# Spreading the key sums z by two 16-row products, and projecting v of tile 14 in the first part

## The chip, the cores and the metric

The kernel runs on one core of a Trainium2 chip. The metric is the device time of one execution in microseconds, as the median of several runs: 389.65 before the change (three runs, 389.32 to 390.35). All times below are in microseconds, and times of the trace count from the start of the span. The engines are named as in the profile: PE is TensorE (PEld its weight loads), DVE is VectorE, ACT is ScalarE, POOL is GpSimd, SP is SyncE, which issues most of the DMAs.

## What is computed

The input x has 2048 rows of 512. Two branches read it and a gate mixes them:

```
g   = sigmoid(sum(x * gate_w))                    # one number per row
out = g * A(x) + (1 - g) * B(x)

A:  q, k, v = x @ wqkv, 32 heads of 16
    phi(t) = [softmax(t @ w_phi), softmax(-(t @ w_phi))]        # 32 features per head
    kv = sum over rows of phi(k)^T v ;  z = sum over rows of phi(k)
    o  = phi(q) kv / (phi(q) . z + 1e-6) ;  A = o @ wo

B:  per row and each of 32 heads: the best of 16 keys k1 and the best of 16 keys k2
    give an expert e = 16 * i1 + i2 ;  B = sum over heads of gelu(x . u[e]) * v[e]
```

z is one number per head and feature, 32 x 32 = 1024 in all. Each row of x needs all of them, multiplied with its own phi(q), so a copy of z has to lie in every one of the 128 partitions.

## The kernel before, in words

The rows are cut into 16 tiles of 128 (`NT`), and the 512 inputs into four blocks of 128 (`NK`). Operands are split into a high and a low part of the type `F32R`: `proj` (L83, over `mm3`, L51) makes twelve products of a tile, for each block high x high (L54), high x low of the weights (L55) and low of x x high (L56). All engines follow an order written out by hand: each engine executes its instructions in the order of the program text, and an instruction that waits holds everything behind it on its engine.

**The first part** (loop at L284) goes over the 16 tiles t. It projects v (`vproj`, into a tile with 17 columns per head, the last of them ones) and k (`kproj`, with w_phi folded into the weights), takes the softmax differences of k on VectorE (`softmax_diffs`, L86), the exponential on ScalarE (L326), and sums and a reciprocal on VectorE and a product on GpSimd (`ksoft`, L177 to L181), and adds phi(k)^T [v, 1] to a PSUM tile `acc` (`kvacc`, L188). Thus column 16 of each head in `acc` gathers z. Beside this the loop builds the score weights `sh`, `sl` of branch B (`score_w`, `score_planes`, `score_join`). Two tiles are treated apart: v of tiles 14 and 15 is not projected here. `kvz` (L192) adds only their z, by products with a column of ones, so that z is complete when the second part begins. In the last pass of the loop the weights of q are folded (`fold`, L133): its products go to PSUM, ScalarE rounds them to `wah` (L137), VectorE subtracts to `wal` (L138). Between its halves stand the scores of tile 0 (`front_s(0, ·)`).

**The bridge** (L627 to L641): `kvz(14)`; `best(0, ·)` finds the maxima of the scores of tile 0 on VectorE (L447) and marks them (L448); `turn_eq(0)` turns the marks by a DMA transpose on SP (L454, tile `et`); `front_q(0)` and `front_p(0)` project tile 0 on q and on u; `soft_in(0)` takes the softmax differences of q on VectorE; `kvz(15)` completes z. Then ScalarE copies z to `zc` (L638), `gelu_pre(0)` prepares the gelu, and `z_final` (L614) spreads z: for each of 8 groups of 128 numbers one 32-bit product of a column of `zc`, broadcast over 128 columns, with the identity (L618), and two copies into `zb` (L620).

**The second part** (loop at L642) runs stage a for tile a, and for n = a + 1, b = a - 1, z = a - 2: in stage a the scores of tile n are made while the softmax of q of tile a is under way, tile b is counted and turned, and tile z is finished and stored. The order of its steps around the change, in stage 0: `gate(0)` (L370) and `gelu_act(0)` (L378 to L380), then `soft_exp(0)` (L403), `mid_mask(0)` on TensorE (L511, reads `et`), `front_s(1, 0)`, `front_s(1, 1)`, `front_p(1)`, `soft_w(0)` on GpSimd (L409, needs `zb`), `soft_sum(0, ·)` (L413), `best(1, 0)`, `soft_y(0, ·)` (L417, needs the product of L409), `soft_b(0)`, `best(1, 1)`. In stage 1 TensorE also projects v of tiles 14 and 15, ScalarE copies them out of PSUM (v15 behind `soft_exp(1)`), and `kvacc(14)` and `kvacc(15)` add their part of phi(k)^T v, without the column of z; then `kv_final` copies `acc` into `kvb`. The weights wo replace those of v in the same tiles, the first two blocks by L670 and L690, the last two, whose loads wait for the buffers of the first, by L702 and L706. From stage 2 on, stage a starts on TensorE with `mid_num` (L491) and `back_c` (L563, the transpose CT of the coefficients that `coef`, L557, leaves).

PSUM is taken by two rings: `mm_bank` (four banks, in order of use) and `tr_bank` (three).

Of the kernel before, what the change touches and what calls it, by code (L numbers as in the profile page):

```python
# [9 lines left out]
F32 = mybir.dt.float32  # L10
F32R = mybir.dt.float32r
# [9 lines left out]
P = 128  # L21
S = 2048
D = 512
# [10 lines left out]
def mix_kernel(ctx, tc, xT, wqT, wkT, wv, wphi, wo, wq, kk, ug, ev, cst, out):  # L34
# [6 lines left out]
    def mm_bank(name):  # L41
        return psum.tile([P, 512], F32, tag="mm", bufs=4, name=name)
# [28 lines left out]
    ones = per.tile([P, 1], F32, name="ones")  # L71
    zc = per.tile([P, 8], F32, name="zc")
    cs = per.tile([P, 160], F32, name="cs")
    ident = cs[:, 0:128]
# [5 lines left out]
    def xs(t, k):  # L80
        return xh[:, t, k, :], xl[:, t, k, :]

    def proj(o, t, wh, wl, c0, c1, ks=range(NK)):  # L83
        mm3(o, [(*xs(t, k), wh[:, k, c0:c1], wl[:, k, c0:c1]) for k in ks], ks[0] == 0, ks[-1] == NK - 1)
# [75 lines left out]
    def vproj(t, ks=range(NK)):  # L160
        if ks[0] > 0:
            return proj(pvs.pop(t), t, wbh, wbl, 0, D, ks)
        pv = pvs[t] = mm_bank(f"pv{t}")
        proj(pv, t, wbh, wbl, 0, D, ks)
        v = vs[t] = home(t).tile([P, H, F + 1], F32, name=f"v{t}", tag="v")
        if t < NT - 2:
            pool.memset(v[:, :, F], 1.0)
        return lambda: act.copy(v[:, :, :F], pv.rearrange("p (h f) -> p h f", f=F))
# [14 lines left out]
    def kvacc(t):  # L183
        n = F + 1 if t < NT - 2 else F
        for g in range(8):
            for c in range(4):
                h = 4 * g + c
                pe.matmul(acc[32 * c:32 * c + 32, g, :n], phis[t][:, 32 * h:32 * h + 32],  # L188
                          vs[t][:, h, :n], start=(t == 0 and g == 0),
                          stop=(t == NT - 1), skip_group_check=True)  # L190
# [33 lines left out]

    def front_s(t, half):
        e = st8[t]
        e[half] = mm_bank(f"s{half}_{t}")
        proj(e[half], t, sh, sl, 512 * half, 512 * half + 512)

# [54 lines left out]
    for t in range(NT):  # L284
        if t + 3 < NT:
            x_load(t + 3)
        if 2 < t < NT - 2:
            vproj(t)()
# [111 lines left out]
    def soft_exp(t):  # L400
        d = st8[t]["ph"]
        for s_ in halves:
            act.activation(d[:, s_], d[:, s_], AF.Exp)  # L403
# [209 lines left out]

    def z_final():  # L614
        for j in range(2):
            o = mm_bank(f"z{j}")
            for g in range(4):
                pe.matmul(o[:, g * P:(g + 1) * P], zc[:, 4 * j + g:4 * j + g + 1].to_broadcast([P, P]), ident,  # L618
                          start=True, stop=True)
            act.copy(zb[:, 512 * j:512 * j + 512], o)  # L620
# [6 lines left out]
    rawo = {}  # L627
    kvz(NT - 2)
    best(0, 0)
# [7 lines left out]
    kvz(NT - 1)  # L637
    act.copy(zc, acc[:, :, F])  # L638
    gelu_pre(0)
    z_final()  # L640
    wo_load((0, 1))  # L641
    for a in range(NT - 1):  # L642
# [8 lines left out]
        if a == 1:  # L651
            v14, v15 = vproj(NT - 2), vproj(NT - 1)
        gelu_in(a)
# [6 lines left out]
        if B:  # L660
            step(b, 4)
            soft_in(a, lambda: step(b, 2))
            drain(b)
        if a == 1:
            v14()
        soft_exp(a)
        if a == 1:
# [8 lines left out]
        mid_mask(a)  # L676
        front_s(n, 0)
        if a == 1:
            kvacc(NT - 2)
            kvacc(NT - 1)  # L680
            cl_.close()
            w4 = ctx.enter_context(tc_pool("w4", "right"))
# [78 lines left out]
def _consts():  # L761
    c = np.zeros((P, 160), np.float32)
    c[:, :128] = np.eye(P, dtype=np.float32)
    p = np.arange(P)
    for q in range(2):
        for a in range(F):
            c[:, 128 + q * F + a] = np.where(p % F == a, 2.0 ** (q * 8 + p // F), 0.0)
    return c
# [42 lines left out]
```

## Time and profile before

| | |
|---|---|
| median of three runs | 389.65 (389.32 to 390.35) |
| the profiled execution | 389.51, its span 387.7 |
| granted TensorE clock, mean over the span | 0.996 |
| first z product (L618) | 135.48 |
| first score product of tile 1 (`front_s(1, 0)`) | 137.57 |
| CT transpose that opens stage 3 (L563) | 177.90 |
| mean bandwidth of the DMAs | 117 GB/s |

The page gives for each engine the time it was busy, for slices of the span the busy tenths, and the chain of work that ended last, followed back from the end: at each step to what released the instruction, or to the one before it on its engine. The timeline gives start, duration, engine, line, operation and tiles; in brackets the idle time before the instruction and what ended it. TensorE's products are pipelined: the shown duration of one is longer than the distance to the next, and a stream is measured by the distances between starts.

### The profile page before, as it was taken

Reading aid. Unit: us, or ns where it says so; the run is one execution under the profiler, and the core shown is the slowest. Engines: PE = TensorE matmul, PEld = TensorE weight load, DVE = VectorE, ACT = ScalarE, POOL = GpSimd, SP = SyncE. Lnnn points to the kernel's source line nnn. Section 1 sums busy time; section 2 is a strip of 40 time slices with the busy share of each in tenths; the row PEclk is TensorE's granted clock in tenths of the full one; section 3 lists DMA queues with packets and bytes.
Section 4 is the critical chain, followed back from the end, with each engine's and each line's share of the span. In section 5 each row is a group of like instructions: output and inputs, shape, how many; then the busy total and the mean of one; then the engine's idle time right before and its main releaser. Section 6 shows DMA issues by size and latency. Waiting matters only on the chain.

```text
span 387.7 us, 9193 instructions
## 1 busy us (share of the span) xinstructions
PE 379.2 (98%) x3688; PEld 296.4 (76%) x3688; DVE 324.3 (84%) x798; ACT 214.2 (55%) x390; POOL 155.9 (40%) x165
## 2 busy tenths in 40 slices
PE   8999999999999999999999999999999999999975
PEld 4866787777768888877878878888888788888753
DVE  4358866866868969889999999999999999999994
ACT  4335555644646345758548458557656664674732
POOL 1005435325326233936426426336335344364350
PEclk9999999999999999999999999999999999999989
DMA  7489787487692033143252231331440431322301
GB/s 272 157 257 313 210 254 231 142 227 238 199 300 57 16 71 81 61 78 81 57 83 60 77 81 50 88 83 34 104 83 28 90 84 48 81 69 69 83 28 56
DMA packets 66715, 45.38 MB, mean 117 GB/s; under 512 B 58096, under 2 KB 58992, under 8 KB 64368
## 3 DMA queue, kind: packets, MB, share of 16 engines
q1 hardware_dynamic: 65808, 43.92, 41.5%
q10 hardware_dynamic: 864, 0.87, 0.8%
q8 instruction: 29, 0.48, 0.5%
q14 instruction: 14, 0.11, 0.1%
HBM read 26.43 MB, written 4.19 MB: 79 GB/s over the span
## 4 chain that ended last, share of the span: by engine, by line
PE 83%; DVE 8%; ACT 3%; DMA 2%; POOL 2%; issue 1%; ACTq 0%; POOLq 0%
PE s L54 7%; PE s L56 6%; PE s L55 6%; PE pk L54 4%; PE ws L204 4%; PE pk L55 4%; PE pk L56 4%; PE pv L54 4%; PE po L578 4%; PE po L579 4%; PE po L584 3%; PE pv L55 3%; PE pv L56 3%; PE pq L54 3%; PE pq L56 3%; PE pq L55 3%
## 5 line engine op out<-in xcount | busy, mean ns | idle before, releaser
L409 POOL TENSOR_TENSOR w<-d,zb 128x512 f32<-128x512 f32 x32 | 40.8, 1299 | 94.6 <-ACT d L403 94.6
L181 POOL TENSOR_TENSOR d<-d,st 128x1024 f32<-128x1024 f32 x16 | 31.0, 1939 | 74.5 <-DVE st L180 38.4
L54 PE MATMUL s<-sh,xh 128*128 128x512 f32 x128 | 51.8, 405 | 0.0
L56 PE MATMUL s<-sh,xl 128*128 128x512 f32 x128 | 50.0, 391 | 0.0
L55 PE MATMUL s<-sl,xh 128*128 128x512 f32 x128 | 49.9, 390 | 0.0
L403 ACT ACTIVATE d<-d 128x512 f32<-128x512 f32 x32 | 18.4, 624 | 56.9 <-DVE d L96 56.9
L439 POOL TENSOR_TENSOR d<-d,st 128x512 f32<-128x512 f32 x31 | 32.7, 1077 | 25.6 <-DVE st L433 20.8
L482 ACT COPY pt<-tp 128x1024 uint16<-128x1024 uint16 x30 | 39.0, 1368 | 1.5 <-DMA tp<-pl 0.9
L326 ACT ACTIVATE d<-d 128x1024 f32<-128x1024 f32 x16 | 17.0, 1063 | 27.9 <-DVE d L96 27.9
L472 ACT COPY pl<-d 128x1024 uint16<-128x1024 uint16 x30 | 30.5, 1061 | 1.6 <-POOL d L439 1.4
L56 PEld LDWEIGHTS s<-sh,xl 128*128 128x128 f32 x128 | 24.0, 188 | 5.4
L413 DVE TENSOR_REDUCE st<-d 128x32 f32<-128x512 f32 x32 | 20.5, 681 | 8.9 <-ACT d L403 8.9
L54 PEld LDWEIGHTS s<-sh,xh 128*128 128x128 f32 x128 | 24.0, 188 | 4.6
L55 PEld LDWEIGHTS s<-sl,xh 128*128 128x128 f32 x128 | 24.1, 188 | 4.5
L578 PE MATMUL po<-wbh,oh 128*128 128x512 f32 x64 | 26.4, 412 | 0.8 <-ACT oh L496 0.8
L54 PE MATMUL pv<-wbh,xh 128*128 128x512 f32 x64 | 26.3, 411 | 0.2 <-ACT wbh L48 0.2
L54 PE MATMUL pq<-wah,xh 128*128 128x512 f32 x64 | 26.5, 415 | 0.0
L579 PE MATMUL po<-wbl,oh 128*128 128x512 f32 x64 | 26.2, 409 | 0.0
L55 PE MATMUL pv<-wbl,xh 128*128 128x512 f32 x64 | 25.4, 396 | 0.2 <-DVE wbl L49 0.2
L179 DVE TENSOR_REDUCE st<-d 128x64 f32<-128x1024 f32 x16 | 19.5, 1218 | 7.0 <-ACT d L326 7.0
L54 PE MATMUL pk<-wah,xh 128*128 128x512 f32 x64 | 25.3, 395 | 0.0
L56 PE MATMUL pv<-wbh,xl 128*128 128x512 f32 x64 | 25.2, 394 | 0.0
(147 smaller groups left out, 1019.9 us busy)
## 6 DMA issues: line engine op xcount, KB each, us to landing
wq<-wq SPq DMA_DIRECT2D x16, 1024.0 KB, 5.9
xr<-xT SPq DMA_DIRECT2D x15, 256.0 KB, 6.1
y<-ot SPq DMA_DIRECT2D x15, 256.0 KB, 2.0
rawk<-wkT SPq DMA_DIRECT2D x1, 1024.0 KB, 6.5
rawq<-wqT SPq DMA_DIRECT2D x1, 1024.0 KB, 4.8
rawo<-wo SPq DMA_DIRECT2D x4, 256.0 KB, 3.7
rawu<-ug SPq DMA_DIRECT2D x2, 258.0 KB, 6.0
rawv<-wv ACTq DMA_DIRECT2D x2, 256.0 KB, 4.6
```

What stands on the lines that cost most here:

```text
L54: pe.matmul(o, ah, bh, start=(first and i == 0), stop=False)
L55: pe.matmul(o, ah, bl, start=False, stop=False)
L56: pe.matmul(o, al, bh, start=False, stop=(last and i == n - 1))
L179: dve.tensor_reduce(st[:, 64:128], g64(d), axis=AX.X, op=ALU.add)
L181: pool.tensor_tensor(g64(d), g64(d), b64(st[:, 128:192]), op=ALU.mult)
L409: pool.tensor_tensor(e["w"][:, s_], e["ph"][:, s_], zb[:, s_], op=ALU.mult)
L413: dve.tensor_reduce(e["st"][:, 64 + 32 * i:96 + 32 * i], g64(e["ph"])[:, 32 * i:32 * i + 32], axis=AX.X, op=ALU.add)
L439: eng.tensor_tensor(g64(d)[:, gs_], g64(d)[:, gs_], r[:, gs_].unsqueeze(2).to_broadcast([P, 32, F]), op=ALU.mult)
L472: act.copy(pl, e["ph"][:, s_].bitcast(U16).rearrange("p (c j) -> p j c", j=2))
L482: act.copy(p16[:, :, 4 * i:4 * i + 4, :], e["tp"][i].rearrange("p (j g) n -> p j g n", j=2))
L578: pe.matmul(po, oh[:, k, :], wbh[:, k, :], start=(k == 0), stop=False)
L579: pe.matmul(po, oh[:, k, :], wbl[:, k, :], start=False, stop=False)
```

## The change

Three edits. First, the z sums are spread in another way. `z_split` copies z from PSUM to `zc`, rounded to the high part, and VectorE writes the remainder beside it: 16 columns. `z_rows` turns them by one TensorE transpose into 16 rows of 128, and VectorE multiplies the rows with a small pattern (from 8 new columns of the constants) into `zm`, 16 rows of 1024, in which each row keeps only its own group of 128. `z_spread` then makes two products of 16 rows with a tile of ones, 512 columns each, which sum high and low part and put the result in all partitions. They stand inside `front_s(1, 0)`, between its second and third block; the transpose stands behind `mid_mask(0)`. `soft_exp(0)` moves out of stage 0 to stand right behind `gelu_pre(0)`.

Second, v of tile 14 is projected in the first part (`vproj(14)` ahead of `kproj(14)`), with its column of ones; `kvacc(14)` with 17 columns takes the place of `kvz(14)`, and both steps leave stage 1.

Third, the projection of v of tile 0 takes, for each block, the low part of x before the low part of the weights.

```diff
@@ -69,8 +69,8 @@
     wbl = per.tile([P, NK, D], F32R, name="wbl")
     kvb = per.tile([P, 8, 32], F32, name="kvb")
     ones = per.tile([P, 1], F32, name="ones")
-    zc = per.tile([P, 8], F32, name="zc")
-    cs = per.tile([P, 160], F32, name="cs")
+    zc = per.tile([P, 16], F32R, name="zc")
+    cs = per.tile([P, 168], F32, name="cs")
     ident = cs[:, 0:128]
     wm = per.tile([P, 2, F], BF16, name="wm")
     kp = per.tile([P, 2, 2, 32], F32, name="kp")
@@ -79,6 +79,13 @@
 
     def xs(t, k):
         return xh[:, t, k, :], xl[:, t, k, :]
+
+    def proj_lo_first(o, t, wh, wl, ks):
+        for i, k in enumerate(ks):
+            (ah, al), h = xs(t, k), wh[:, k, :]
+            pe.matmul(o, ah, h, start=(i == 0), stop=False)
+            pe.matmul(o, al, h, start=False, stop=False)
+            pe.matmul(o, ah, wl[:, k, :], start=False, stop=(i == len(ks) - 1))
 
     def proj(o, t, wh, wl, c0, c1, ks=range(NK)):
         mm3(o, [(*xs(t, k), wh[:, k, c0:c1], wl[:, k, c0:c1]) for k in ks], ks[0] == 0, ks[-1] == NK - 1)
@@ -161,9 +168,12 @@
         if ks[0] > 0:
             return proj(pvs.pop(t), t, wbh, wbl, 0, D, ks)
         pv = pvs[t] = mm_bank(f"pv{t}")
-        proj(pv, t, wbh, wbl, 0, D, ks)
+        if t == 0:
+            proj_lo_first(pv, t, wbh, wbl, ks)
+        else:
+            proj(pv, t, wbh, wbl, 0, D, ks)
         v = vs[t] = home(t).tile([P, H, F + 1], F32, name=f"v{t}", tag="v")
-        if t < NT - 2:
+        if t < NT - 1:
             pool.memset(v[:, :, F], 1.0)
         return lambda: act.copy(v[:, :, :F], pv.rearrange("p (h f) -> p h f", f=F))
 
@@ -181,7 +191,7 @@
         pool.tensor_tensor(g64(d), g64(d), b64(st[:, 128:192]), op=ALU.mult)
 
     def kvacc(t):
-        n = F + 1 if t < NT - 2 else F
+        n = F + 1 if t < NT - 1 else F
         for g in range(8):
             for c in range(4):
                 h = 4 * g + c
@@ -222,10 +232,11 @@
 
     st8 = {t: {} for t in range(NT)}
 
-    def front_s(t, half):
-        e = st8[t]
-        e[half] = mm_bank(f"s{half}_{t}")
-        proj(e[half], t, sh, sl, 512 * half, 512 * half + 512)
+    def front_s(t, half, ks=range(NK)):
+        e = st8[t]
+        if ks[0] == 0:
+            e[half] = mm_bank(f"s{half}_{t}")
+        proj(e[half], t, sh, sl, 512 * half, 512 * half + 512, ks)
 
     pool.memset(warm, 0.0)
     tab = w1.tile([P, 1], F32, bufs=1, name="tab")
@@ -284,7 +295,7 @@
     for t in range(NT):
         if t + 3 < NT:
             x_load(t + 3)
-        if 2 < t < NT - 2:
+        if 2 < t < NT - 1:
             vproj(t)()
         kproj(t)
         old = [] if t == NT - 3 else list(joins)
@@ -611,12 +622,26 @@
             r = slice(32 * c, 32 * c + 32)
             act.copy(kvb[r, :, F * (c % 2):F * (c % 2) + F], acc[r, :, :F])
 
-    def z_final():
+    def z_split():
+        act.copy(zc[:, :8], acc[:, :, F])
+        dve.tensor_tensor(zc[:, 8:], acc[:, :, F], zc[:, :8], op=ALU.subtract)
+
+    def z_rows():
+        o = mm_bank("zT")
+        pe.transpose(o[:16, :P], zc.bitcast(F32), ident)
+        one = w2.tile([16, P], F32R, name="one", bufs=1)
+        dve.tensor_copy(one, ones[:16].to_broadcast([16, P]))
+        zm = w2.tile([P, 1024], F32R, tag="w", bufs=1, name="zm")[:16].rearrange("p (g n) -> p g n", n=P)
+        for j in range(2):
+            js = slice(4 * j, 4 * j + 4)
+            dve.tensor_tensor(zm[:, js], o[:16, :P].unsqueeze(1).to_broadcast([16, 4, P]),
+                              cs[:16, 160:168][:, js].unsqueeze(2).to_broadcast([16, 4, P]), op=ALU.mult)
+        return one, zm
+
+    def z_spread(one, zm):
         for j in range(2):
             o = mm_bank(f"z{j}")
-            for g in range(4):
-                pe.matmul(o[:, g * P:(g + 1) * P], zc[:, 4 * j + g:4 * j + g + 1].to_broadcast([P, P]), ident,
-                          start=True, stop=True)
+            pe.matmul(o, one, zm[:, 4 * j:4 * j + 4].rearrange("p g n -> p (g n)"), start=True, stop=True)
             act.copy(zb[:, 512 * j:512 * j + 512], o)
 
     def wo_load(ks):
@@ -625,7 +650,7 @@
             sp.dma_start(rawo[k], wo[:, k, :])
 
     rawo = {}
-    kvz(NT - 2)
+    kvacc(NT - 2)
     best(0, 0)
     best(0, 1)
     cb.close()
@@ -635,9 +660,9 @@
     soft_in(0)
     front_p(0, False)
     kvz(NT - 1)
-    act.copy(zc, acc[:, :, F])
+    z_split()
     gelu_pre(0)
-    z_final()
+    soft_exp(0)
     wo_load((0, 1))
     for a in range(NT - 1):
         n, b, z = a + 1, a - 1, a - 2
@@ -649,7 +674,7 @@
             planes(b)
             front_q(a)
         if a == 1:
-            v14, v15 = vproj(NT - 2), vproj(NT - 1)
+            v15 = vproj(NT - 1)
         gelu_in(a)
         if Z:
             num_lo(z)
@@ -661,9 +686,8 @@
             step(b, 4)
             soft_in(a, lambda: step(b, 2))
             drain(b)
-        if a == 1:
-            v14()
-        soft_exp(a)
+        if a > 0:
+            soft_exp(a)
         if a == 1:
             v15()
             for k in range(2):
@@ -674,9 +698,14 @@
             back_out(z)
             store(z)
         mid_mask(a)
-        front_s(n, 0)
+        if a == 0:
+            zrow = z_rows()
+            front_s(n, 0, range(2))
+            z_spread(*zrow)
+            front_s(n, 0, range(2, NK))
+        else:
+            front_s(n, 0)
         if a == 1:
-            kvacc(NT - 2)
             kvacc(NT - 1)
             cl_.close()
             w4 = ctx.enter_context(tc_pool("w4", "right"))
@@ -759,9 +788,10 @@
 
 
 def _consts():
-    c = np.zeros((P, 160), np.float32)
+    c = np.zeros((P, 168), np.float32)
     c[:, :128] = np.eye(P, dtype=np.float32)
     p = np.arange(P)
+    c[:16, 160:] = np.tile(np.eye(8, dtype=np.float32), (2, 1))
     for q in range(2):
         for a in range(F):
             c[:, 128 + q * F + a] = np.where(p % F == a, 2.0 ** (q * 8 + p // F), 0.0)
```

## The prediction

> **What bounds the kernel now.** I read the page first, its busy shares and the summary of the chain that ended last.
>
> ```profile
> PE 379.2 (98%) x3688; PEld 296.4 (76%) x3688; DVE 324.3 (84%) x798; ACT 214.2 (55%) x390; POOL 155.9 (40%) x165
> PE 83%; DVE 8%; ACT 3%; DMA 2%; POOL 2%; issue 1%; ACTq 0%; POOLq 0%
> ```
>
> TensorE carries 83% of the chain, so work taken from it looks like time gained. But the other 17% lie together. The same chain in order of time, from the end of the first part, shows where:
>
> ```profile
> 137.56 0.59 ACT zb L620
> 139.75 1.28 DVE st L413 x2
> 141.03 0.61 DVE mx L447
> ...
> 157.18 2.59 POOL wbl L690 x2
> 159.79 3.01 DMA rawo<-wo
> 162.82 0.62 ACT wbh L702
> ...
> 177.12 0.74 POOL cf L557
> 177.90 0.44 PE CT L563 x2
> ```
>
> From 137.6 to 177.9 the chain runs over ScalarE, VectorE, GpSimd and a DMA; only at the transpose CT that opens stage a = 3 does it come back to TensorE, which carries it from there nearly to the end. So what the change is worth is decided by two things: when VectorE starts `best(1,0)` (141.03 in the chain, its reduction issued at 140.94), and whether anything between there and CT can catch up. The stretches answer the second:
>
> ```profile
> core 0: us, PE busy (x) PEld busy (x) DVE busy (x) ACT busy (x) POOL busy (x), PEclk, DMA share, GB/s
> 115.10:130.10 15.00, 15.00 (x425) 12.55 (x411) 13.81 (x21) 9.92 (x13) 6.35 (x4) 1.00 0.25 65
> 137.50:152.80 15.30, 15.30 (x82) 12.68 (x79) 12.77 (x34) 7.65 (x17) 5.35 (x6) 1.00 0.34 79
> ```
>
> TensorE has no hole in either (first busy column equals the length), and VectorE works 12.77 of 15.30; of the 2.5 it rests there, 2.25 lie before 139.75 (last row of the VectorE fence below, idle 3.45 before it).
>
> **The change part by part.** *v of tile 14 moved.* Twelve products leave stage a = 1 and go in front of the k projection of tile 14 (111.1). Their cost is the distance of two such groups in the TensorE timeline, 150.02 - 147.27 = 2.75:
>
> ```profile
> 134.48 0.71 PE L196 MATMUL kvacc<-ones,d 128*32 128x1 f32 x64
> 135.48 2.05 PE L618 MATMUL z<-cs,zc 128*128 128x128 f32 x16 [0.28 <-ACT zc L638]
> 137.36 0.35 PE L511 MATMUL mk<-wm,et 128*128 128x16 bf16 x8
> 137.57 0.47 PE L54 MATMUL s<-sh,xh 128*128 128x512 f32 x1
> 140.15 0.39 PE L56 MATMUL s<-sh,xl 128*128 128x512 f32 x1
> 147.27 0.39 PE L54 MATMUL pv<-wbh,xh 128*128 128x512 f32 x1
> 150.02 0.39 PE L54 MATMUL pv<-wbh,xh 128*128 128x512 f32 x1
> 155.95 1.27 PE L188 MATMUL kvacc<-v,d 128*32 128x16 f32 x128
> ```
>
> TensorE is full there, so nothing hides them: all of its queue up to the z sums comes 2.75 later. `kvacc(14)` with 17 columns takes the place of `kvz(14)` at about the same price: both kinds are 64 instructions, in 0.7 (the row at 134.48) and 0.64 (half of the 128 at 155.95). In stage a = 1 TensorE is rid of 2.75 + 0.64. The copy of v14 (0.57, the v15 row below) moves into a long rest of ScalarE's, and the memset is one more small GpSimd step; I take both as nothing.
>
> Does VectorE follow those 2.75? Its queue and ScalarE's at the place:
>
> ```profile
> L137 ACT CAST wah<-foldq 128x512 fp32r<-128x512 f32 x4 | 2.1, 601 | 2.3 <-PE foldq L147 2.3
> 126.02 2.06 ACT L137 CAST wah<-foldq 128x512 fp32r<-128x512 f32 x4 [2.25 <-PE foldq L147]
> 127.06 2.47 DVE L138 TENSOR_TENSOR wal<-foldq,wah 128x512 fp32r<-128x512 f32 x4
> 133.91 1.23 SPq L454 DMA_TRANSPOSE et<-eq  x1
> et<-eq SPq DMA_TRANSPOSE x1, 3.0
> 135.55 0.68 DVE L96 TENSOR_TENSOR d<-st,pq 128x512 f32<-128x512 f32 x1
> 136.31 0.42 ACT L365 ACTIVATE x<-x 128x256 f32<-128x256 f32 x1
> 139.75 1.28 DVE L413 TENSOR_REDUCE st<-d 128x32 f32<-128x512 f32 x2 [3.45 <-ACT d L403]
> ```
>
> The first `wah` waits for the second half of the q fold, so it comes 2.75 later. It is out at 126.02 + 0.60 = 126.62, VectorE takes it up at 127.06: 0.44 to spare. So `wal`, and behind it in VectorE's queue `ksoft(15)`, `best(0,·)` and `soft_in(0)`, move by 2.75 - 0.44 = 2.3. VectorE has one rest to make that good, the 3.45 ahead of 139.75, in which it waits for the exponential that stood behind the z copies. Moving `soft_exp(0)` forward aims at it: `gelu_pre(0)` ends at 136.73 + 2.75 = 139.5, `soft_in(0)` at 136.23 + 2.3 = 138.5, so the first half of d is out at 139.5 + 0.62 = 140.1.
>
> *z spread anew.* The 2.05 of z go, and with them a cover that the page does not name. `turn_eq(0)` lands at 133.91 + 3.0 = 136.9, while z kept TensorE busy until 137.36, so `mid_mask(0)` never waited. In the new order nothing stands between `kvz(15)`, over at about 135.2 + 2.75 = 138.0, and the mask, and et lands at 136.9 + 2.3 = 139.2: TensorE stands for 1.2, with everything behind the mask. From the mask's start to the end of the twelve s products took 140.15 + 0.39 - 137.36 = 3.2, and 0.1 more to VectorE's start. Into that come one transpose (the CT pair in the chain took 0.44; I take 0.15, bounds 0.1 and 0.4) and two 16-row products (no row here has this shape; a 128-row one has a pitch of 2.75 / 12 = 0.23, a 128-row z piece 2.05 / 16 = 0.13; I take 0.23 each plus 0.1 for the change of shape, bounds 0.26 and 0.9 for the two). That is 0.7. `best(1,0)` can start at 139.2 + 3.3 + 0.7 = 143.2, against 140.94: **+2.3**.
>
> Is TensorE the later one? VectorE adds the subtraction and the copy, in the rest, and two 16 x 512 multiplies out of PSUM, which I price as the 128 x 512 row (L96, 0.68; a pair, by the L413 row, 1.28). They start when the transpose is out, 139.2 + 0.2 + 0.15 + 0.3 = 139.9, and end at 141.2; two sums of 1.2 in all (139.75 to 140.94) follow, to 142.4. VectorE alone would be at +1.4; the scores end later, so +2.3 holds. zb is no later: its products start six s products (1.5) behind the transpose, at 141.0, are done at 141.8, and two copies of 0.59 (L620 in the chain) follow, to 143.0. GpSimd's first half of w (the next row: half of 2.54) then ends near 143.7, and `soft_y` wants it behind `best(1,0)`, at 143.2 + 1.3 = 144.5.
>
> ```profile
> 139.85 2.54 POOL L409 TENSOR_TENSOR w<-d,zb 128x512 f32<-128x512 f32 x2 [2.32 <-ACT d L403]
> ```
>
> SyncE's queue comes 2.3 later as well, `turn_eq(0)` and behind it the first two wo loads; those are read in stage 1 only, ten microseconds on, so nothing waits for them.
>
> *The rest of the way to CT.* From `best(1,0)` on the chain quoted above has no term that the change shortens: VectorE's queue loses nothing in stages 0 and 1, `soft_exp(1)`, the w product, L690, the wo DMA and L702 follow each other as before. TensorE's 3.4 saved are spent waiting:
>
> ```profile
> 155.04 0.57 ACT L168 COPY v<-pv 128x512 f32<-128x512 f32 x1
> ```
>
> v15 is copied behind `soft_exp(1)`, so at 155.6 + 2.3 = 157.9; TensorE would be at `kvacc(15)` by 155.7: from the first s product to it were 155.95 - 137.57 = 18.4, of which 2.75 go and 0.7 come, behind a mask that ends at 139.4. It stands there about 2.2, with the second half of tile 2's scores, its projection on u and `mid_num(0)` queued behind; none of them is late for it, since what they feed hangs on VectorE's and ScalarE's queues, 2.3 behind too. At CT it waits again for cf.
>
> *Low part of x first in v of tile 0.* Nothing. The next projection is held by `xl` of tile 1, whatever the first one's order:
>
> ```profile
> 9.38 0.19 PEld L55 LDWEIGHTS pv<-wbl,xh 128*128 128x128 f32 x1 [0.24 <-DVE wbl L49]
> 9.70 0.69 DVE L129 TENSOR_TENSOR xl<-xr,xh 128x512 fp32r<-128x512 f32 x1
> 10.45 0.50 PE L56 MATMUL pv<-wbh,xl 128*128 128x512 f32 x1
> ```
>
> The last wait for `wbl` (until 9.38) stays, one product fewer follows it, and the 0.23 gained end at the xl product, which cannot start before 9.70 + 0.69 = 10.39.
>
> Sum: 2.3 to 2.5 behind CT, and TensorE is the chain from there. The profiled run took 389.5 (span 387.7 plus 1.8 around it), 0.1 under the median of 389.65; 389.65 + 2.35 gives **392.0**.
>
> **The rivals.** *TensorE's sum decides (faster).* From the end of `kvz(15)` (135.2) to the mask (137.36) were 2.2, against 0.7 new, and `kvacc(14)` was 0.64: 2.1 less work, 387.6. It needs cf not to hold CT. For it: 98% busy and 83% of the chain. Against it: the chain at 177.12, where cf ends 0.04 before CT starts.
>
> *VectorE takes up the whole shift (no change).* If et came early and the sums started within a microsecond of 139.75: 389.7, up to 390.4. Against it: d is not out before 140.1 and the multiplies stand ahead of the sums.
>
> *Only VectorE's own queue counts.* If TensorE is not held at the mask, +1.4: 391.0.
>
> *The clock halves.* The tail of this trace shows a half clock behind a thin stretch:
>
> ```profile
> 367.59:371.00 3.41, 1.34 (x28) 0.69 (x21) 3.02 (x9) 2.60 (x7) 1.83 (x2) 1.00 0.01 2
> 371.00:374.42 3.42, 3.42 (x10) 2.64 (x9) 3.31 (x13) 0.15 (x1) 2.07 (x3) 0.50 0.20 77
> ```
>
> 1.34 busy of 3.41, then 3.42 at clock 0.50. After the mask wait a stretch of that length has about 2.2 busy, after the wait for v15 about 1.2. A drop at the second place costs TensorE up to 1.7, most of which it would spend waiting anyway (+0.3); at the first it lands on the scores for `best(1,0)`, by half of that in the mean: 392.9, and at most 393.7. The Trainium skill (TensorE: Matmul & The Clock Gate, "Why this matters for your kernels") asks only that idle gaps stay under about 3 us; by that no drop comes here and the time is 392.0. The trace does not bear that out fully: its drop followed waits of at most 1.56 between thin products.
>
> **How the numbers follow.** The forecast (391.6 to 392.9, with the bounds of the transpose and the two products and a drop at the second place) gets 0.62, VectorE's queue alone 0.10, the halved clock at the scores 0.06, no change 0.12, TensorE's sum 0.10. A run can tell 0.3%, 1.2 us, from nothing. Slower: 0.62 + 0.10 + 0.06 = 0.78; same 0.12; faster 0.10. The range 389.9 to 393.3 leaves out the faster case, half of the unchanged one and the top of the clock case.
>
> **What would show it.** Right: `wal` near 129.4; TensorE idle a good 1 us before the mask products, released by the et DMA; `best(1,0)` near 143.3; an idle of about 2 before `kvacc(15)`, released by the v15 copy; the CT that opens stage 3 near 180.3; a pitch of 15.2 from there on. Wrong: `best(1,0)` before 142, or TensorE at CT before cf is there.

## The result and the profile after

The changed kernel takes 396.53 us (median of four runs, 395.66 to 396.99); the kernel before, run beside it, 390.0 (four runs, 389.32 to 391.07). The ratio is 1.0157, with a 95% interval of 1.0135 to 1.0179: some 6.1 us slower. The forecast was 392.0 with a range up to 393.3, so the sign was right, and the loss was more than twice what was summed up. The profiled execution took 396.99, its span 395.2.

The page of the changed kernel: TensorE's row, the row of granted clock over 40 slices, and the summary of the chain by engine.

```profile
PE 382.7 (97%) x3611; PEld 297.2 (75%) x3611; DVE 327.6 (83%) x802; ACT 214.1 (54%) x390; POOL 156.5 (40%) x166
...
PEclk9989999999999979999999999999999999999989
...
PE 80%; DVE 10%; ACT 3%; DMA 3%; issue 2%; POOL 2%; ACTq 0%; POOLq 0%; SPq 0%
```

TensorE has 77 products fewer (3688 before) and is nonetheless busy 3.5 us longer (379.2 before). Fewer products that take longer mean a lower clock, and the clock row shows where: a 7 in the fifteenth slice, which is 138 to 148 us, right after the bridge, an 8 in the third (20 to 30 us), and an 8 near the end, which the kernel before has as well. The mean clock fell from 0.996 to 0.983.

Three places carry the loss. The first lies at the end of the first part. The timeline of the changed kernel there, start, duration, engine, and in brackets the idle time before and what ended it:

```profile
119.55 1.01 ACT L219 COPY wpl<-ws 128x1024 uint16<-128x1024 uint16 x1 [2.42 <-issue]
121.85 1.25 SPq L221 DMA_TRANSPOSE wtp<-wpl  x1
126.28 1.37 ACT L226 COPY wtj<-wtp 128x1024 uint16<-128x1024 uint16 x1 [2.85 <-DMA wtp<-wpl]
128.21 1.14 ACT L48 CAST eh<-rawe 128x512 fp32r<-128x512 f32 x2
128.38 1.28 POOL L231 TENSOR_TENSOR sl<-wtj,sh 128x512 fp32r<-128x512 f32 x1 [4.54 <-ACT sh L230]
128.86 3.70 DVE L49 TENSOR_TENSOR el<-rawe,eh 128x512 fp32r<-128x512 f32 x2 [1.25 <-ACT eh L48]
129.61 2.39 POOL L191 TENSOR_TENSOR d<-d,st 128x1024 f32<-128x1024 f32 x1
132.47 2.47 DVE L145 TENSOR_TENSOR wal<-foldq,wah 128x512 fp32r<-128x512 f32 x4
```

`wal` is at 132.47, not near 129.4. Ahead of it in VectorE's queue stands `el`, the low part of another weight, the expert values v[e] (`split`, L48 and L49), and VectorE idles 1.25 ahead of it, for its high part `eh`. `eh` stands on ScalarE behind the copy `wtj`, and that waits 2.85 for a DMA transpose. The same instructions in the timeline of the kernel before, four to five and a half microseconds earlier and without a wait for the DMA, and with them GpSimd's product d at that place:

```profile
115.24 1.01 ACT L209 COPY wpl<-ws 128x1024 uint16<-128x1024 uint16 x1 [0.16 <-ACT uh L48]
117.53 1.25 SPq L211 DMA_TRANSPOSE wtp<-wpl  x1
120.72 1.35 ACT L216 COPY wtj<-wtp 128x1024 uint16<-128x1024 uint16 x1
122.63 1.13 ACT L48 CAST eh<-rawe 128x512 fp32r<-128x512 f32 x2
124.05 1.94 POOL L181 TENSOR_TENSOR d<-d,st 128x1024 f32<-128x1024 f32 x1
124.85 2.28 DVE L49 TENSOR_TENSOR el<-rawe,eh 128x512 fp32r<-128x512 f32 x2
```

The second place is the mask, and what follows it. The same timeline:

```profile
139.17 0.71 PE L206 MATMUL kvacc<-ones,d 128*32 128x1 f32 x64
139.33 1.24 SPq L465 DMA_TRANSPOSE et<-eq  x1
142.10 0.36 PE L522 MATMUL mk<-wm,et 128*128 128x16 bf16 x8 [2.22 <-DMA et<-eq]
142.72 0.63 PE L55 MATMUL s<-sl,xh 128*128 128x512 f32 x1
143.15 0.63 PE L56 MATMUL s<-sh,xl 128*128 128x512 f32 x1
144.99 1.22 PE L644 MATMUL z<-zm,one 16*128 16x512 f32 x2
149.10 0.69 DVE L458 TENSOR_REDUCE mx<-s 128x32 f32<-128x512 f32 x1 [3.58 <-PE s L56]
163.75 0.74 PE L198 MATMUL kvacc<-v,d 128*32 128x16 f32 x64 [1.74 <-ACT v L178]
185.93 0.44 PE L574 MATMUL CT<-cs,cf 128*128 128x128 f32 x2 [0.20 <-POOL cf L568]
```

TensorE stands for 2.22 before the mask, released by the et DMA: the wait that the prediction named, with 1.2 in place of 2.2. Then the score products come every 143.15 - 142.72 = 0.43 us, where before their distance was 0.23. `best(1,0)` starts at 149.10 (140.94 before), VectorE having idled 3.58 for the scores, and the CT that opens stage 3 at 185.93 (177.90 before): 8.0 later. From there on nothing more is lost: the spans differ by 395.2 - 387.7 = 7.5.

The third place is the clock itself. Stretches of the changed kernel; the columns are length, busy time (instructions) of PE, PEld, DVE, ACT and POOL, granted clock, DMA share and GB/s:

```profile
core 0: us, PE busy (x) PEld busy (x) DVE busy (x) ACT busy (x) POOL busy (x), PEclk, DMA share, GB/s
139.14:142.56 3.42, 1.20 (x75) 1.09 (x75) 3.15 (x8) 2.29 (x8) 0.73 (x1) 1.00 0.46 94
142.56:145.97 3.41, 3.41 (x9) 1.88 (x7) 2.46 (x4) 1.42 (x5) 0.00 (x0) 0.50 0.53 144
145.97:149.38 3.41, 3.41 (x9) 2.57 (x9) 0.28 (x1) 0.92 (x2) 2.52 (x2) 0.50 0.00 0
16.27:19.68 3.41, 3.41 (x69) 3.05 (x69) 1.15 (x4) 1.07 (x4) 0.00 (x0) 1.00 0.00 0
...
19.68:23.09 3.41, 3.41 (x9) 2.67 (x9) 0.76 (x3) 0.72 (x2) 0.00 (x0) 0.50 0.83 318
```

The stretch with the mask wait is busy 1.20 of 3.42; the two behind it, which hold all but the start of the first half of the scores, run at half clock, nine products each. Another halved stretch lies at 19.68, behind one in which TensorE was busy throughout. It made everything after it later: the first `ws` products, 1.5 us behind its end, start at 24.64 where before they start at 23.08, and the eight `ws` products that open the work on tile 14 at 111.66, where before they start at 110.11. These 1.55 come ahead of the moved products. Of the experiments' profiles only one (e5) shows a halved stretch there; still, the `ws` of tile 14 start between 110.08 and 111.49 in the others. So below, positions are compared "net": less the kernel's own start of `ws` and 110.11.

### The profile page after: what moved, and what is told of

Read it like the earlier page. It is cut to its first block, busy times and chain, and to the rows that moved or that the text cites. A ratio compares the mean times of both kernels' runs of the same rounds, so it can differ in the third digit from the quotient of the medians.

```text
span 395.2 us, 9043 instructions
## 1 busy us (share of the span) xinstructions
PE 382.7 (97%) x3611; PEld 297.2 (75%) x3611; DVE 327.6 (83%) x802; ACT 214.1 (54%) x390; POOL 156.5 (40%) x166
## 4 chain that ended last, share of the span: by engine, by line
PE 80%; DVE 10%; ACT 3%; DMA 3%; issue 2%; POOL 2%; ACTq 0%; POOLq 0%; SPq 0%
PE s L54 6%; PE s L55 6%; PE s L56 6%; PE pv L54 4%; PE po L589 4%; PE ws L214 4%; PE po L590 3%; PE pk L54 3%; PE pk L55 3%; PE pk L56 3%; PE pv L56 3%; PE po L595 3%; PE pv L55 3%; PE pq L56 3%; PE pq L54 3%; PE pq L55 3%
## 5 line engine op out<-in xcount | busy, mean ns | idle before, releaser
L54 PE MATMUL s<-sh,xh 128*128 128x512 f32 x128 | 52.7, 412 | 0.0
L55 PE MATMUL s<-sl,xh 128*128 128x512 f32 x128 | 50.9, 398 | 0.0
L56 PE MATMUL s<-sh,xl 128*128 128x512 f32 x128 | 50.8, 397 | 0.0
L55 PE MATMUL pk<-wal,xh 128*128 128x512 f32 x64 | 25.5, 399 | 0.0
L56 PE MATMUL pk<-wah,xl 128*128 128x512 f32 x64 | 25.5, 399 | 0.0
L458 DVE TENSOR_REDUCE mx<-s 128x32 f32<-128x512 f32 x32 | 21.9, 683 | 4.3 <-PE s L56 3.6
L56 PE MATMUL pq<-wah,xl 128*128 128x512 f32 x64 | 25.3, 395 | 0.0
```

Of the source, the lines that this page charges most:

```text
L54: pe.matmul(o, ah, bh, start=(first and i == 0), stop=False)
L55: pe.matmul(o, ah, bl, start=False, stop=False)
L56: pe.matmul(o, al, bh, start=False, stop=(last and i == n - 1))
L458: dve.tensor_reduce(mx, p3, axis=AX.X, op=ALU.max)
```

## The experiments

Theory: the loss is the `el` behind the DMA, plus the exposed et wait, plus a half clock behind that wait. Rivals: the bare move of v14, the new z or the edit of the first projection cost this by themselves; or the clock falls because the new products have only 16 rows, not because TensorE stands still. The time at half clock in a run, wherever it lies, is 2 x (1 - mean clock) x span: 10.2 to 13.4 us in all four runs of the changed kernel, 0 to 4.7 in the runs of the kernel before, whose profile has one halved stretch of 3.41, in the tail.

### Which of the three edits costs

**e2_v14_only**: the kernel before with the move of v14 alone.

```diff
...
-        if 2 < t < NT - 2:
+        if 2 < t < NT - 1:
             vproj(t)()
...
-    kvz(NT - 2)
+    kvacc(NT - 2)
...
-            v14, v15 = vproj(NT - 2), vproj(NT - 1)
+            v15 = vproj(NT - 1)
...
-            kvacc(NT - 2)
             kvacc(NT - 1)
```

> The kernel before with the move of v of tile 14 alone; the 32-bit z products stay behind kvz(15). Theory: the first part is 2.75 us longer on TensorE, the marks of tile 0 come 3.9 us later (el behind wtj of the last score block and beside GpSimd), the z products cover all but about 0.8 us of the wait for et, no half clock: best(1,0) at +2.75 to +3.3, time 392.8 to 393.3. Rival (what the first part gains in length stage 1 gives back): 389.5 to 390.5.

Measured: 393.62 (392.04 to 394.54), ratio 1.009 (1.0064 to 1.0115), some 3.5 us and 0.3 above the theory's range. `wal` stands at 131.18. Timeline at the bridge:

```profile
138.85 2.05 PE L618 MATMUL z<-cs,zc 128*128 128x128 f32 x16 [0.28 <-ACT zc L638]
141.12 0.36 PE L511 MATMUL mk<-wm,et 128*128 128x16 bf16 x8 [0.22 <-DMA et<-eq]
144.35 0.69 DVE L447 TENSOR_REDUCE mx<-s 128x32 f32<-128x512 f32 x1
```

The old z products cover the DMA all but 0.22, and `best(1,0)` is 3.4 later than before. The move of v14 alone is thus more than half of the loss. It also brings the wait for v15: 2.04 before `kvacc(15)` and, in this profile, a halved stretch behind it (160.12 to 163.53).

**e3_z_only**: the new z with the early `soft_exp(0)`, v14 and the first projection as before.

```diff
...
-    kvacc(NT - 2)
+    kvz(NT - 2)
...
-            v15 = vproj(NT - 1)
+            v14, v15 = vproj(NT - 2), vproj(NT - 1)
...
+        if a == 1:
+            v14()
...
+            kvacc(NT - 2)
             kvacc(NT - 1)
```

> The changed kernel with v of tile 14 left in stage 1 and the first v projection as before: the new z and the early soft_exp(0) alone. Theory: kvz(15) ends near 135.2, et lands near 137.0, so TensorE stands about 1.7 us; best(1,0) near 141, as before, time 390 if the clock holds, 391.5 to 393 with a half clock behind the wait. Rival (TensorE's sum decides): 1.5 us less work, 388.3.

Measured: 390.71 (ten runs, 388.96 to 393.19), ratio 1.0023 (1.0 to 1.0045). The mask row of its timeline, and in a second fence two stretches:

```profile
136.89 0.36 PE L519 MATMUL mk<-wm,et 128*128 128x16 bf16 x8 [1.51 <-DMA et<-eq]
```

```profile
core 0: us, PE busy (x) PEld busy (x) DVE busy (x) ACT busy (x) POOL busy (x), PEclk, DMA share, GB/s
133.74:137.15 3.41, 1.90 (x83) 1.68 (x81) 2.95 (x8) 1.64 (x7) 0.16 (x1) 1.00 0.41 85
137.15:140.56 3.41, 3.41 (x13) 2.30 (x10) 2.46 (x4) 1.81 (x5) 0.57 (x1) 0.50 0.56 148
```

Without z's old products the mask waits here too, 1.51, though et comes as early as before; and a stand of 1.51, in a stretch still busy 1.90, was followed by a halved one. Three of the ten runs had some 10 us at half clock and took 391.95 to 393.19; two with 7 us, the profiled one among them, took 390.59 and 391.06; the five with 3 to 4 us took 388.96 to 390.84. So the new z alone costs little or nothing (0 to 1.8 us by the interval), and the rival by TensorE's sum (388.3) is out.

**e9_lo_only**: the kernel before with the first projection's new order alone.

```diff
...
-        proj(pv, t, wbh, wbl, 0, D, ks)
+        if t == 0:
+            proj_lo_first(pv, t, wbh, wbl, ks)
+        else:
+            proj(pv, t, wbh, wbl, 0, D, ks)
```

> The kernel before with the new order of the first v projection alone. Theory: nothing, 390.0 to 390.9 as before, since xl of tile 1 holds the next projection. Rival (it is this order that brings the half clock near 20 us which the changed kernel's profile shows): a second halved stretch in some of the runs, and in these 1.5 us more.

Measured: 390.69 against 390.9, ratio 0.9988 (0.9974 to 1.0001): nothing that can be told from no change, and no run had more than 4.7 us at half clock. So this edit alone does not bring the early halved stretch either.

### Does TensorE's stand at the mask halve the clock?

**e1_keep_warm**: the changed kernel, with ten more products into a PSUM bank that nobody reads, where TensorE would stand. They are added work.

```diff
     kvz(NT - 1)
+    fill = tr_bank("fill")
+    for _ in range(10):
+        pe.matmul(fill, xh[:, 0, 0, :], wah[:, 0, :], start=True, stop=True)
```

> The changed kernel with ten 128x512 products into an unused bank between kvz(15) and the mask products, so that TensorE works through the wait of 2.2 us for et instead of standing. Theory (the thin stretch halves the clock): no half clock at the mask, the s products of tile 1 at their 0.23 pitch, best(1,0) about 3 us earlier against the mask than in the changed kernel; time 393.1 where the changed kernel has 396.1 to 396.5. Rival (the 16-row z products or the z steps themselves bring the clock down): the half clock stays or comes a stretch later, time above 395.

Measured: 393.75 (392.99 to 394.04), ratio 1.0087 (1.0061 to 1.0112). Work was added and the kernel became faster, by 0.0157 - 0.0087 = 0.0070 or 2.7 us. The timeline:

```profile
138.85 2.57 PE L665 MATMUL fill<-wah,xh 128*128 128x512 f32 x10
141.27 0.36 PE L522 MATMUL mk<-wm,et 128*128 128x16 bf16 x8
145.71 0.69 DVE L458 TENSOR_REDUCE mx<-s 128x32 f32<-128x512 f32 x1 [1.01 <-PE s L56]
```

From the mask to `best(1,0)` are 4.44, where the changed kernel took 149.10 - 142.10 = 7.00: the difference, 2.56, agrees with the ratios. All four runs have 3.1 to 3.9 us at half clock. In the profile that stretch lies behind the wait for v15:

```profile
157.83:161.24 3.41, 1.44 (x68) 0.99 (x67) 3.03 (x6) 2.56 (x5) 1.85 (x2) 1.00 0.00 0
161.24:164.66 3.42, 3.42 (x9) 2.67 (x9) 3.41 (x7) 3.37 (x7) 3.42 (x4) 0.50 0.09 23
```

**e7_keep_warm16**: the same ten products with 16 rows instead of 128.

```diff
-        pe.matmul(fill, xh[:, 0, 0, :], wah[:, 0, :], start=True, stop=True)
+        pe.matmul(fill, xh[:16, 0, 0, :], wah[:16, 0, :], start=True, stop=True)
```

> As the first experiment, ten products of 512 columns through the wait for et, but of 16 rows instead of 128. Theory A (the clock goes by how much of the array works): thin, half clock behind the mask as in the changed kernel, time about 396. Theory B (it goes by whether products run at all): full clock at the mask, time 393.7 as with 128 rows.

Measured: 394.61 (four runs, 393.19 to 397.35), ratio 1.0112 (1.0077 to 1.0147).

```profile
139.75 2.58 PE L665 MATMUL fill<-wah,xh 16*128 16x512 f32 x10
142.26 0.36 PE L522 MATMUL mk<-wm,et 128*128 128x16 bf16 x8
```

The mask and the scores ran at full clock in this profile: from the mask to `best(1,0)` (146.68) are 4.42, as in e1. Three of the runs had 3.1 to 7.1 us at half clock; the fourth, the 397.35, had 10.3, and where it lay is not known. The interval overlaps that of e1 and also that of the changed kernel, so the time does not tell the two theories apart; the profile speaks for B. The rows of the changed kernel say more about the rival of the 16-row products: its half clock begins at 142.56, 2.4 ahead of the first of them (144.99), so they did not bring it. Whether they prolonged it is not shown; in e3 the first of them starts at 139.97, inside the halved stretch, and the next stretch is at full clock.

**e4_z_after**: the two 16-row products behind the twelve score products instead of amid them.

```diff
-            front_s(n, 0, range(2))
+            front_s(n, 0)
             z_spread(*zrow)
-            front_s(n, 0, range(2, NK))
```

> The changed kernel with the two 16-row products behind the twelve s products instead of between them. Theory A (16-row products count as thin and keep the half clock for a second stretch): one stretch at half clock at the mask instead of two, best(1,0) near 147 instead of 149.1, time about 394.1 where the changed kernel has 396.1. Theory B (the second stretch has nothing to do with them): two stretches again, best(1,0) about 1.4 us earlier only because the products are out of the way, time about 394.8.

Measured: 395.34 (394.38 to 396.32), ratio 1.0131 (1.0101 to 1.0161). That fits neither theory's time, and the interval overlaps that of the changed kernel. In its profile the mask waited 2.23, just as in the changed kernel, and no halved stretch followed, not even the first, which the move cannot have prevented: it changes only what stands behind the scores (the last section returns to this). zb came late instead, and VectorE stood 1.0 and 0.56 for `soft_y`, waiting for the w product. So the run does not tell the two theories apart. It gave one useful price:

```profile
144.51 0.73 PE L644 MATMUL z<-zm,one 16*128 16x512 f32 x2
145.16 0.50 PE L54 MATMUL s<-sh,xh 128*128 128x512 f32 x1
```

Without a wait between them, the two take 145.16 - 144.51 = 0.65.

### Is it el that made wal later than forecast?

**e6_el_early**: the changed kernel, with the split of that weight one tile earlier, ahead of the exponential of tile 14.

```diff
         if t == NT - 2:
             score_join(*old.pop())
-        elif t == NT - 1:
             for k in range(2):
                 split(eh[:, k, :], el[:, k, :], rawe[k])
+        elif t == NT - 1:
             fq = fold(rawq, wah, wal, "q", False)
```

> The changed kernel with the split of the expert values (eh on ScalarE, el on VectorE) one tile earlier, ahead of the exponential of tile 14, where both engines rest. Theory: wal no longer stands behind el, which stood behind the last score join and beside GpSimd; wal starts 2.3 to 2.7 us behind the kernel before instead of 4.1 to 4.5, et 1.7 us earlier, TensorE waits about 1.4 us at the mask instead of 2.2; time 392.5 if that no longer halves the clock, 394.5 if it does. Rival (el has no part in it): 396.

Measured: 391.7 (ten runs, 391.37 to 393.29), ratio 1.0034 (1.0018 to 1.005). The moved split brings back 4.8 of the 6.1 us, the half clock at the mask among them. The timeline:

```profile
121.76 1.96 DVE L49 TENSOR_TENSOR el<-rawe,eh 128x512 fp32r<-128x512 f32 x2 [1.80 <-ACT eh L48]
129.68 2.49 DVE L145 TENSOR_TENSOR wal<-foldq,wah 128x512 fp32r<-128x512 f32 x4 [1.91 <-ACT wah L144]
139.36 0.36 PE L522 MATMUL mk<-wm,et 128*128 128x16 bf16 x8 [1.11 <-DMA et<-eq]
143.78 0.69 DVE L458 TENSOR_REDUCE mx<-s 128x32 f32<-128x512 f32 x1 [0.99 <-PE s L56]
158.43 0.74 PE L198 MATMUL kvacc<-v,d 128*32 128x16 f32 x64 [2.00 <-ACT v L178]
180.59 0.44 PE L574 MATMUL CT<-cs,cf 128*128 128x128 f32 x2 [0.19 <-POOL cf L568]
```

With `el` out of the way every position that the prediction gave is there within 0.6: `wal` 129.68 (129.4), a mask wait of 1.11 (1.2), `best(1,0)` at 143.78 (143.2), a v15 wait of 2.00 (2.2), CT at 180.59 (180.3). And in this profile no halved stretch follows the mask; seven of the ten runs had 3.1 us at half clock, two 7.0 and one 10.2.

**e10_v14_el**: e2 with the same move of the split, so the bare price of moving v14. Against e2, the diff is that of e6.

> The move of v of tile 14 together with the earlier split of the expert values, the old z. Theory: the bare price of twelve products on a full TensorE ahead of a chain that stage 1 does not shorten: wal at 2.3 to 2.7, et inside the cover of the z products, best(1,0) at 2.75 behind, 392.6 to 393.4 where the kernel before has 390.0 to 390.8. Rival (the loss of the move was el's lateness alone): 390.8 or less.

Measured: 393.65 (392.72 to 393.85), ratio 1.0069 (1.0051 to 1.0087): 2.7 us. That is 0.25 above the theory's range and far from the rival's 390.8: the move of v14 has a price of its own, without `el`. The intervals of e2 (1.009) and e10 overlap, so beside the old z the early split is not shown to help. e6, which differs from e10 by the new z and the first projection's order, has 1.0034, so beside the moved v14 the new z gains some 1.4 us, though the two intervals only just part.

### Can the new z bring anything?

**e5_mask_later**: the changed kernel, with all scores of tile 1 ahead of the mask, the transpose of z behind their first half and the two products inside their second.

```diff
-        mid_mask(a)
         if a == 0:
+            front_s(n, 0)
             zrow = z_rows()
-            front_s(n, 0, range(2))
+            front_s(n, 1, range(2))
             z_spread(*zrow)
-            front_s(n, 0, range(2, NK))
+            front_s(n, 1, range(2, NK))
+            mid_mask(a)
         else:
+            mid_mask(a)
             front_s(n, 0)
...
```

The PSUM tiles of zT and z come from the ring `tr_bank` in this kernel, in e8 and in e11.

> The changed kernel with the mask products behind all scores of tile 1, the transpose of z behind its first half and the z products inside its second half (in the other PSUM ring), so that nothing on TensorE waits for et. Theory (exposed et and the half clock behind it cost 3 to 4 of the 6.3 us, the longer first part the rest): no wait over 0.5 us and full clock there, best(1,0) at about 3 us behind the kernel before, time 393.0 to 393.5. Rival (the lateness of VectorE out of the first part alone gives the loss): 395 or more.

Measured: 393.48 (393.1 to 395.68), ratio 1.0071 (1.0047 to 1.0095). The mask no longer waits, but VectorE now waits for zT, and TensorE stands 2.94 before `kvacc(15)`, a halved stretch behind it. Moving the wait away from the mask takes the half clock there away, and the time is as forecast; what stays is the size of e10, the price of v14. Its profile is the one other with a halved stretch near 20 us (20.05 to 23.46).

**e8_z_mask_later**: the new z with v14 where it was (as e3), zT between the halves of `front_s(1, 0)`, the two products behind it and the mask behind them.

```diff
...
-        mid_mask(a)
         if a == 0:
-            zrow = z_rows()
             front_s(n, 0, range(2))
-            z_spread(*zrow)
+            zrow = z_rows()
             front_s(n, 0, range(2, NK))
+            z_spread(*zrow)
+            mid_mask(a)
         else:
+            mid_mask(a)
             front_s(n, 0)
...
```

> The new z and the early soft_exp(0) without the move of v, with the mask products behind z and z behind the first half of tile 1's scores, in the other PSUM ring. Theory: nothing on TensorE waits for et, best(1,0) at 139.6 to 140.2 instead of 140.9, no half clock outside the tail, time 389.0 (0.8 to 1.4 us less than before). Rival (zb, now later than d, holds soft_y as much as is gained): 390.

Measured: 389.01 (twelve runs, 388.28 to 390.3) against 390.85, ratio 0.996 (0.9944 to 0.9975): faster than the kernel before, by 1.6 us.

```profile
139.66 0.36 PE L519 MATMUL mk<-wm,et 128*128 128x16 bf16 x8
140.29 0.67 DVE L455 TENSOR_REDUCE mx<-s 128x32 f32<-128x512 f32 x1
177.51 0.44 PE L571 MATMUL CT<-cs,cf 128*128 128x128 f32 x2 [0.18 <-POOL cf L565]
```

No wait stands before the mask, and VectorE starts `best(1,0)` without a rest: the scores are no longer what it waits for (it has one rest of 0.83 earlier, for zT). CT is 0.4 earlier than before, net 0.9. Beside the mask's place, that of z and its PSUM ring changed against e3, so the gain is not divided among them.

**e11_z_mask_later_el**: e8 and the early split together.

> The version of e8 with the expert values split one tile earlier as well. Theory: wal no longer waits behind el and starts with wah, 0.4 us earlier than in e8; what follows on VectorE comes 0.4 us earlier: 388.6 where e8 had 389.0 (before 390.0 to 390.9). Rival (the exponential of tile 14, now behind the split, gives it back): 389.0.

Measured: 388.86 (twelve runs, 387.96 to 390.68) against 390.9, ratio 0.996 (0.9943 to 0.9977). The split brings nothing more here that a run can tell. `wal` does start 0.46 earlier net (126.73 against 127.64 in e8), but VectorE then waits 1.17 for zT where e8 waits 0.83, and `best(1,0)` starts at the same net 139.76 in both.

## Why the prediction was right or wrong

**The sum, closed.** The net positions account for the 8.03 between the two CTs:

| step | measured | from |
|---|---|---|
| the prediction's own chain (v14, et wait, z products) | 2.40 | e6: 180.59 - 177.90, less 0.29 of start |
| `el` ahead of `wal` | 1.53 | net shift of `wal`: 3.86 changed, 2.33 in e6 |
| half clock from the mask to `best(1,0)` | 2.58 | 7.00 changed, 4.42 in e6 |
| later start (110.11 to 111.66) | 1.55 | profile of the changed kernel |
| sum | 8.06 | |

The rows are read from single profiles. By the measured ratios the same split is 1.3 us for e6 (0.7 to 2.0), 2.1 from there to e1 and 2.7 from e1 to the changed kernel, 6.1 in all. So over all runs the first row is about half of what the profiles show, and less than the 2.35 forecast. Two things bear on it: the profiled run of before (389.51) stands 1.3 under the median of the runs beside e6 (390.85), and of the 2.69 between the two CTs 2.2 are left at the end of the span. The later start is not part of every run and is in no forecast.

**TensorE's gain does not come through; VectorE's chain to CT decides.** Right. At CT TensorE still waits for cf (the bracket of its row), and it stands 1.74 before `kvacc(15)` (2.2 forecast). The rival that TensorE's sum decides is out: 77 products fewer, and slower.

**"`wal`, and behind it in VectorE's queue `ksoft(15)`, `best(0,·)` and `soft_in(0)`, move by 2.75 - 0.44 = 2.3."** This is the first step that failed. It followed one input of `wal`, the fold, and not what stands ahead of `wal` on its engine. The second half of the `ws` products comes 2.75 later too; with it the copy `wpl` (net 119.55 - 115.24 - 1.55 = 2.76), the DMA transpose behind it and `wtj`. In the kernel before, that DMA was issued at 117.53 and `wtj` ran at 120.72 without waiting, so it took at most 3.2; in the changed kernel it took 4.36 (121.85 to 126.21). So `eh` came 4.0 later net (128.21 - 122.63 - 1.55). And the slack of 0.44 was no free time: in the kernel before `wal` already stood behind `el`, which ended at 124.85 + 2.28 = 127.13. Net, `wal` came 3.86 later in place of 2.3. e6 shows that `el` is the reason: without it at that place the shift is 2.33. The late `wal` made the wait for et longer than forecast, and with it the thin stretch that the half clock followed. With that wait filled and full clock at the mask (e1) the kernel still takes 393.75, just above the range; the rest is the clock, below.

**Most of the extra 1.5 looks like a lock, not a queue.** Net, `el` started only 128.86 - 124.85 - 1.55 = 2.46 later; the other 1.42 is its length, 3.70 for two pieces in the changed kernel against 2.28 in the kernel before (1.96 in e6). GpSimd's `sl` and d, which hang on the same DMA, came 4.0 later net (d 129.61 - 124.05 - 1.55), so that `el` now met both where it had met d alone. Its first piece ended 0.55 behind `sl` (128.38 + 1.28 = 129.66), its second, at 132.55, 0.55 behind d (129.61 + 2.39 = 132.00), and d itself took 2.39 in place of 1.94. The Trainium skill (SBUF — State Buffer, "SBUF: two separate sides") says that a VectorE operation with two SBUF inputs and a GpSimd operation that reads SBUF exclude each other for a whole instruction; the rows here agree. No run takes the two apart: e6 removes the queue and the lock together.

**The et wait of 1.2.** The mechanism was right, and the size follows from the step above: 2.22 in the changed kernel, 1.11 in e6, where `wal` came as forecast. z's old products were indeed a cover; e2, which keeps them, waits 0.22.

**The transpose and two 16-row products, 0.7 in all.** A size was off. From the mask to `best(1,0)` e6 took 4.42, where 3.3 + 0.7 = 4.0 was forecast. The pair itself takes 0.65 (e4) for a forecast of 0.56; amid the scores it takes longer, since its second product stands behind the second half of VectorE's multiplies.

**The clock that halves, at 0.06.** This is the second step that failed, in its chance and its size. The mechanism was there as a rival, with the place and a price of 0.9 in the mean, at most one stretch. In the profile it came, and two stretches long: 2.6 to 2.7 us. The other three runs had 10.2 to 11.9 us at half clock, about three stretches where the profile of before has one, so it probably came in them too, though the mean clock does not say where. The prediction reckoned with 2.2 busy in the stretch of the mask wait; with the late `wal` it was 1.20. And "at the first it lands on the scores for `best(1,0)`, by half of that in the mean" led astray: the drop began 0.46 behind the mask's start and stayed for nearly the whole of the scores. The Trainium skill (TensorE: Matmul & The Clock Gate, "Why this matters for your kernels") asks that idle gaps stay under about 3 us; behind waits of 2.22 and, in e3, of 1.51 the clock halved here, so the measurement decides against relying on that figure.

**The low part of x first: nothing.** Right (e9).

**What stays open.** Why the DMA transpose took 4.36 in place of 3.2. Why the half clock lasted two stretches in the changed kernel and one in e3. Why a stretch near 20 us was halved though TensorE was busy all through the one before it: most of that one are 64 small products of the k fold (32 rows, 32 columns), but in the kernel before the same products fill a stretch (16.02 to 19.43), and full clock follows. And the exact threshold: stretches busy 1.20, 1.38, 1.44 and 1.90 of 3.41 were followed by half clock; in e6 one of 1.55 was not.

## What to carry to other kernels

Before a long instruction is taken off a full engine, look what lands while it runs: here it hid a DMA that everything behind it needs, and putting independent products ahead of the waiting one (e8) turned the new z from no gain (e3, 1.0023) into a gain (0.996). When work is moved ahead of a chain on another engine, follow every instruction that stands ahead of that chain in its queue, its inputs and their DMAs, and not only the chain's own input. A stand of TensorE of 1.5 to 2.2 us may cost more than its own length: the clock can be halved behind it, and in the changed kernel that cost 2.7, more than the wait.

## What the hardware showed unexpectedly

The half clock comes in stretches of 3.41 us on a fixed grid within a run. In the changed kernel those at 19.68, 142.56 and 145.97 all begin 2.61 behind a multiple of 3.413; in the kernel before the one at 371.01 begins 2.37 behind one, in e3 (137.15) 0.62, in e1 (161.24) 0.81. So the same wait falls differently on the grid in each run.

How busy TensorE was within one stretch of that grid goes with the clock of the next. Each profile cut on its own grid, the thirteen of them have 20 stretches busy 0.88 to 1.90 of 3.41; half clock follows 18 of these (not the 1.55 in e6 and one of 1.65 near the end of e5), and, where the clock is on record, none of those busy 1.93 to 2.98. The wait of 2.22 in the changed kernel fell into one stretch and left it 1.20; the wait of 2.23 in e4 lay across a boundary, at 140.20, left the two stretches 2.33 and 2.27, and no half clock followed. This fits that e3 and e6 had more half clock in some runs than in others, and it makes the size of the loss in part a matter of luck. No run moved the phase alone, so that the phase decides is argued, not shown.

Ten products of 16 rows took 142.26 - 139.75 = 2.51, ten of 128 rows 141.27 - 138.85 = 2.42: the rows that a product sums over hardly change its time.
